# A gated mix of a long convolution and a token mixer on one core: halves of the token tensors loaded in pairs from one queue, zeros between tap products, and a new hand-written order

## The chip, the cores and the metric

The kernel runs on one core of a Trainium2 chip. TensorE (PE in the profile) multiplies matrices into PSUM; VectorE (DVE), ScalarE (ACT) and GpSimd (POOL) compute on SBUF and empty PSUM; SyncE (SP) computes nothing and issues most of the DMAs. The metric is the device time of one execution in microseconds (us), the median of several runs.

## The reference

Inputs are bf16, with S = 2048 tokens and D = 640 channels. x is the tensor q. Cut to what matters:

```python
g = sigmoid((x * gate_w).sum(-1, keepdims=True))
# branch a: a 4-tap shift convolution, a product, a convolution over all 2048 tokens, a gate by q
k_shift = sum over t of k_pad[:, t:t + S, :] * shift_k[:, 3 - t]
kv = k_shift * v
y  = irfft(rfft(kv padded to 2S) * rfft(ssm_k padded to 2S))[:S] + kv * ssm_D
a  = x * y
# branch b: a token-shift mixer and an MLP
h  = gelu(layernorm(x) @ w1)           # 640 -> 640
hs = concat(h shifted by +1, -1, +2, -2 tokens, a quarter of the channels each) @ w2
x1 = x + hs
b  = x1 + gelu(layernorm(x1) @ w3) @ w4    # 640 -> 1536 -> 640
out = g * a + (1 - g) * b
```

The long convolution is done as a Fourier transform in two steps, written as matrix products with small tables of sines.

## The kernel before, in words

Tokens lie on partitions in a folded way: token number is 32n + 16g + s, partition is 64g + n (g is 0 or 1), and s (0 to 15) counts "slots". So one slot is a tile of 128 tokens by 640 channels, and a load of some slots is made of two **halves**, g = 0 for partitions 0 to 63 and g = 1 for partitions 64 to 127, a DMA each.

`build` (line 354) writes the work as some 780 tasks. Each has an engine (or a choice of engines), the buffers that it takes and gives back, and a function that issues its instructions. The tasks are issued in the order of the list `ORDER`, written out by hand above the code: numbers of tasks, with a letter where the engine is chosen (a is ACT, v is DVE, p is POOL). Every engine and every queue works strictly in that order. `Plan.place` (line 147) goes through the same list with estimated costs, only to choose buffers and the number of **fills**: matmuls of zeros (line 255) into a spare bank that keep PE busy while it would wait.

The stages, with the names and lines of the kernel before:

- Head: tables of sines (POOL, DVE lines 414 to 447, ACT line 451). Tap weights are spread over partitions by PE (`cjb`, line 464, one partition's row times ones) and copied to SBUF (`cj`). x is loaded (`ldx`, line 476), its statistics are made on DVE (lines 513 to 515) or ACT (519, 520), finished on POOL (526 to 528), it is normalized (`nm1`, 532 or 534), transposed by PE (`tr1`, 540) and copied out of PSUM (`ev1`). The filter ssm_k is loaded in 5 blocks (`ldsk`, line 489) and transposed by PE (`trh`, line 754, 32 matmuls a block).
- First mixer: `w1` (615, 619) with gelu on ACT (632), `w2` (641), and `x1` on DVE (648), which adds to x.
- Tap stage, on DVE alone: for each of four groups of four slots (`kv3` first, `kv0` last) 4 products with tap weights (774), 3 sums (778) and the product with v (782): 8 passes over 2560 elements.
- First Fourier step: `s1h` on the filter and `s1x` on the four groups of kv (809, 822), copied to SBUF, written to DRAM and read back in another order (834, 848).
- MLP: layernorm of x1, transposed by DMA (`dt2`, 716), `w3` (724) with gelu (731), `w4` (738), `t2` on DVE (744).
- Second Fourier step and back: `s2` (856), products on DVE (871), `s3` (884), to DRAM and back (896, 916).
- End: `s4` (934), `yq` (940, times q, which is loaded again, 922), `ad` (946), store (955).

All loads and stores but six are on SP's queue; the six g = 1 halves of x are on ACT's. K is loaded in four pieces of 4 slots (`ldk`, 493), v likewise (`ldv`, 767), both as halves of 4 slots (320 KB each); x in halves of 2 or 4 slots. SP holds at most 8 DMAs in flight: each issue waits for the DMA eight issues before it.

PSUM has 8 banks; a fill keeps one bank until the first `w1`, and most tasks take a pair.

Of the kernel before, what the change touches and what calls it, by code (L numbers as in the profile page):

```python
# [10 lines left out]
ACT = mybir.ActivationFunctionType  # L11
ALU = mybir.AluOpType
BF16 = mybir.dt.bfloat16
# [3 lines left out]
P = 128  # L17
D = 640
# [18 lines left out]
0 4 3 17 20 19 63p 8 22 23 24 30 54v 28 73p 2 5 1 55 26 21 74v 64v 56a 18 37 33 57 59v 76a 77 66v 75 36 7 11 35  # L37
9 10a 13 79v 15 12a 58v 16a 390 14a 40 396 65 25 78v 80 67 82v 34 41 83 29 39 6 391a 68v 69v 81v 84a 60 62v 31
70 71v 86v 61a 394 397a 122 27 38 85 87v 32 92v 93 395a 88 90a 114v 126 123 115 42 89v 127 91 116v 100v 118v 47
398 392 130 45 399v 98a 124 117 101 131 94a 125 128 49 72v 95v 119v 43 99 129 96 106v 393a 97v 108v 400 120 132  # L40
107 102a 51 103a 133 109 121a 138 139 135 136 134 104 110v 441 111v 453 454a 141 442a 105v 112 142 44 144 449
403 455 48 113a 461 404 405 406 407 408 166 145 168 450a 172 462a 402 46 456a 169 173 443 444a 459 170 167 460a
146 401 171 53 174 152 445 147 447 457 175 153 52 409 414 410 148 458a 137 446a 448a 214 150 151 182 176 149 464
413 415 215 177 183 216a 463 179 180 140 157 451 452 185 143 217 465 473 158 220 163 181 186 159 474a 466a 188
471 416 189 412 164 411 469 477 196 50 221 470a 192 224v 225 218v 478v 472a 197 417 418 467 483 485 193 419 468a
190 486a 191 194 160 484a 154 420 481 161 219 476 165 479 475 195 198 222v 421 155 162 264 424 480a 482a 199 223
422 178 201 202 207 489 156 423 258 487 497 490a 265 208 302 210 211 259 262v 491 498a 268v 495 266a 488 492a
212 204 226 230 425 260a 501 205 213 496a 426 227 231 493 494a 509 242 701 303 261 712 244 236 502a 427 228 702
243 507 510a 245 500 304v 237 508a 713 505 263 503 428 504a 240 506a 429 232 499 269 241 267 434 233 229 246 238
248 430 433 435 513 517 436 437 511 438 431 432 247 239 249 515 516a 234 270 235 439 252 512 518a 514a 271 187  # L50
521 522a 305 519 520a 440 280 253 281 290 525 291 527 306v 526v 529 274 530a 531 528v 184 533 276 308 250 534a
206 200 532v 282 203 524 309 307 523 209 312v 310v 277 535 346 347 352 251 275 536 286 697v 256 283 313 311 353
356v 537 287 542 257 254 558 553 272 538 354a 543 348v 350a 255 539v 574 540 292 273 622 544a 559 541a 545 288
546a 278 289 560v 547 284 293 279 548 554 556 285 569 349 561 555v 557a 562a 563 564 585 590 294 575 576a 295
549 551v 314 355 550a 570 357 577 315 572 606 316 571v 573v 601 578a 317 591 593 649 592a 326 320 579 565 594a
327 324 586 580 321 566a 567v 325 588 589a 587v 552 336 607 595 351 337 602 596 604 605v 322 608a 318 603a 633
597 323 599v 609 617 328 618 319 598a 332 610a 620 568 329 611 623 612 334 624v 619a 654 681 650 651v 621a 333
652 625 626v 330 653a 335 581 331 582a 627 655 670 628 583a 342 656a 634 635a 613 343 636 657 614v 658v 638 639
600 615a 584 659 660 637a 629 641 640a 665 344 630a 616 642a 643 644 345 686 671 631a 632 672a 666 667v 668 687
688v 669a 689 682 684 685v 690a 661 683a 662a 645 663v 673 675 674a 646a 647a 676 298 691 677 648 299 698 678a  # L60
679a 692 664 693 680 694v 695a 296 300 340 301 297 699a 358 341 696 711 714 717 700 370 718 715 722 706 703 707
# [22 lines left out]
class Plan:  # L84
# [62 lines left out]
    def place(self, order):  # L147
        tasks = self.tasks
        n = len(tasks)
        free = {e: 0.0 for e in LAT}  # L150
# [5 lines left out]
        for i in order:  # L156
            t = tasks[i]
            e = t.on
# [63 lines left out]
def kernel(  # L222
# [16 lines left out]
    nc = tc.nc  # L239
# [8 lines left out]
    with tc.manual_schedule():  # L248
        nc.vector.memset(env.early("FZ", [P, 512], BF16)[:], 0.0)
# [104 lines left out]
def build(env, nc, io):  # L354
    pl = Plan()
    add = pl.add
# [17 lines left out]
    def dma(name, nbytes, fn, issue=0.58, queue="SP", **kw):  # L374
        return add(name, queue, issue, fn, nbytes=nbytes, **kw)
# [79 lines left out]
    fill = add("fill", "PE", 0.02, lambda t: None, acq=[ONE], mode="f")  # L455
# [18 lines left out]
    for (s0, s1) in [(14, 16), (0, 2), (2, 4), (4, 8), (8, 12), (12, 14)]:  # L474
        for g in range(2):
            dma(f"ldx{s0}.{g}", 64 * (s1 - s0) * D * BF * 1.2, lambda t, s0=s0, s1=s1, g=g: (nc.scalar if g else nc.sync).dma_start(
                out=env["x"][64 * g:64 * g + 64, s0:s1, :], in_=qv[g, :, s0:s1, :]), queue="ACT" if g else "SP",
                w=[("x", s, g) for s in range(s0, s1)])
# [12 lines left out]
    for (i0, i1) in ((15, 19), (11, 15), (7, 11), (3, 7)):  # L491
        for g in range(2):
            dma(f"ldk{i0}.{g}", 64 * (i1 - i0) * D * BF * HALF, lambda t, i0=i0, i1=i1, g=g: nc.sync.dma_start(
                out=env["K"][64 * g:64 * g + 64, i0:i1, :], in_=kv_[g, :, i0 - 3:i1 - 3, :]),
                w=[("K", i, g) for i in range(i0, i1)], roles=("K",))
    dma("ldkh1", 64 * 3 * D * BF * 2, lambda t: nc.sync.dma_start(out=env["K"][64:128, 0:3, :], in_=kv_[0, :, 13:16, :]),
        w=[("K", i, 1) for i in range(3)], roles=("K",))
    dma("ldkh0", 64 * 3 * D * BF * 2, lambda t: nc.sync.dma_start(out=env["K"][1:64, 0:3, :], in_=kv_[1, 0:63, 13:16, :]),
        w=[("K", i, 0) for i in range(3)], roles=("K",))
# [265 lines left out]
    for gi in (3, 2, 1, 0):  # L765
        for g in range(2):
            dma(f"ldv{gi}.{g}", 64 * 4 * D * BF * HALF, lambda t, gi=gi, g=g: nc.sync.dma_start(
                out=env["VC"][64 * g:64 * g + 64, 0, :, :], in_=vv[g, :, 4 * gi:4 * gi + 4, :]), w=[("V", g)], roles=("VC",))
# [144 lines left out]
    for s0 in range(0, 16, 2):  # L913
# [4 lines left out]
        qown = None  # L918
        for g in range(2):
            def ldq(t, s0=s0, g=g, o=qown):  # L920
                b = (o or t).buf["Q"][0]
                nc.sync.dma_start(out=env["QO"][64 * g:64 * g + 64, 2 * b:2 * b + 2, :], in_=qv[g, :, s0:s0 + 2, :])
            kw = dict(acq=("Q",), after=("W12",)) if qown is None else {}
            t = dma(f"ldq.{s0}.{g}", 64 * 2 * D * BF * HALF, ldq, use=[qown] if qown else [], w=[("q", s0, g)], **kw)
            qown = qown or t
        oown = None
        for i in range(2):
# [14 lines left out]
            y = add(f"yq.{s}", "DVE", 0.88, yq, use=[t], rel=[(t, "U"), (qown, "Q")], r=["GG", ("q", s0, 0), ("q", s0, 1)], acq=("V",),  # L942
# [6 lines left out]
            o = add(f"ad.{s}", "DVE", 0.75, ad, use=[y] + ([oown] if oown else []), rel=[(y, "V")], r=["GG", ("x", s, 0), ("x", s, 1)],  # L949
                    w=[("o", s)], after=("W12",), **kw)  # L950
            oown = oown or o
        for g in range(2):
            def st(t, s0=s0, g=g, o=oown):
                b = 4 + 2 * o.buf["O"][0]
                nc.sync.dma_start(out=ov[g, :, s0:s0 + 2, :], in_=env["QO"][64 * g:64 * g + 64, b:b + 2, :])
            dma(f"st.{s0}.{g}", 64 * 2 * D * BF * HALF, st, r=[("o", s0), ("o", s0 + 1)], rel=[(oown, "O")])
# [32 lines left out]
```

## Time and profile before

| | us |
|---|---|
| median of 3 runs (238.21 to 238.35) | 238.26 |
| the profiled execution, own time | 238.23 |
| its span, first to last instruction | 236.5 |
| PE, DVE, ACT, POOL busy | 220.1, 185.9, 158.2, 36.8 |
| first `w1` matmul / first tap pass / last tap pass ends | 27.01 / 45.60 / 109.36 |
| last `s1x` group starts on PE / last matmul ends about | 111.38 / 230.5 |

A line of the chain or of a timeline gives the start in us from the span's first instruction, the length, the engine, what it writes, its source line and the number of instructions merged. A line of the windows gives a stretch, its length, then for PE, PEld (weight loads), DVE, ACT and POOL the busy time and number of instructions in it, then PE's granted clock (1.00 is full), the mean busy share of the 16 DMA engines, and GB/s. A busy PE includes the fills.

### The profile page before, as it was taken

The page shows a single profiled execution, that of the slowest core. Times are in us where ns is not written, and L with a number is a line of the kernel's source. Part 1 is how long each engine was busy: PE and PEld are TensorE (multiplying, and loading weights), DVE is VectorE, ACT ScalarE, POOL GpSimd, SP SyncE. Part 2 cuts the span into 40 slices and gives each one's busy share as a digit, 9 for nine tenths or more (in the row PEclk, how much of TensorE's full clock was granted, in tenths as well). Part 3 has the DMA queues.
Part 4 walks back from the last instruction along what each step waited for, and adds up shares of the span by engine and source line. Part 5 has one row for each costly group of instructions (what it writes and reads, how often), then busy time and mean ns, then how long its engine had stood idle before and what let it go on. Part 6 is the DMA issues. An engine that isn't in the chain of part 4 may idle for free.

```text
span 236.5 us, 5276 instructions
## 1 busy us (share of the span) xinstructions
PE 220.1 (93%) x2135; PEld 109.7 (46%) x2154; DVE 185.9 (79%) x263; ACT 158.2 (67%) x221; POOL 36.8 (16%) x91
## 2 busy tenths in 40 slices
PE   8489799999999999999999999999879999999990
PEld 2147576634544564444554343334345654454550
DVE  6926696899999989996754888897999327787892
ACT  0995989998699797887963868897976702522000
POOL 8553364000530330000240000000000000000000
PEclk9679999999999989999999999999999999999997
DMA  6999999998998956985999699987851876877942
GB/s 169 206 224 286 288 214 194 229 335 309 358 243 197 257 199 160 271 236 149 320 259 387 205 237 276 259 283 269 262 192 36 316 258 238 294 218 244 266 112 55
DMA packets 37429, 56.23 MB, mean 238 GB/s; under 512 B 13467, under 2 KB 28572, under 8 KB 37404
## 3 DMA queue, kind: packets, MB, share of 16 engines
q1 hardware_dynamic: 36924, 54.57, 80.2%
q10 hardware_dynamic: 480, 1.31, 2.4%
q8 instruction: 17, 0.28, 0.5%
q14 instruction: 8, 0.07, 0.1%
HBM read 34.90 MB, written 18.35 MB: 225 GB/s over the span
## 4 chain that ended last, share of the span: by engine, by line
PE 76%; DMA 13%; DVE 3%; issue 2%; ACT 2%; SPq 1%; ACTq 0%; DVEq 0%
PE PS L724 23%; PE PS L738 16%; PE PS L641 9%; PE PS L615 8%; DMA x<-in_A_q_dram 6%; DMA W<-in_B_w_dram 5%; PE PS L884 4%; PE PS L856 4%; PE PS L809 4%; DMA QO<-in_A_q_dram 2%; PE PS L619 2%; PE PS L754 2%; PE PS L934 2%; DVE W L940 1%; PE PS L540 1%
## 5 line engine op out<-in xcount | busy, mean ns | idle before, releaser
L738 PE MATMUL PS<-W,h2T 128*128 128x128 bf16 (+1 forms) x372 | 53.6, 297 | 0.6
L731 ACT ACTIVATE h2T<-PS 128x512 bf16<-128x512 f32 x48 | 27.8, 605 | 29.6 <-PE PS L724 29.0
L738 PEld LDWEIGHTS <-h2T 128*128 128x128 bf16 x384 | 29.9, 98 | 25.9 <-issue 2.3
L379 ACT CAST FS<-PS 128x1024 bf16<-128x1024 f32 x36 | 35.1, 1017 | 3.6 <-PE PS L809 2.4
L724 PEld LDWEIGHTS <-W 128*128 128x128 bf16 x240 | 21.9, 99 | 30.2 <-issue 8.7
L379 ACT CAST XH<-PS 128x1024 bf16<-128x1024 f32 x26 | 25.6, 1018 | 5.9 <-PE PS L856 4.2
L724 PE MATMUL PS<-x1nT,W 128*128 128x512 bf16 x120 | 29.5, 392 | 0.0
L724 PE MATMUL PS<-XB,W 128*128 128x512 bf16 x120 | 28.3, 380 | 0.0
L774 DVE TENSOR_TENSOR VC<-K,VC 128x2560 bf16<-128x2560 bf16 x16 | 23.7, 1489 | 0.3
L871 DVE TENSOR_TENSOR PP<-XH 128x2048 bf16<-128x2048 bf16 x20 | 23.6, 1220 | 0.5 <-ACT XH L379 0.2
L744 DVE TENSOR_TENSOR x<-PS,x 128x640 bf16<-128x640 f32 x16 | 13.1, 822 | 13.4 <-PE PS L738 13.2
L641 PE MATMUL PS<-W,hsT 128*128 128x128 bf16 (+1 forms) x155 | 23.2, 302 | 0.3
L615 PE MATMUL PS<-xnT,W 128*128 128x512 bf16 x80 | 19.0, 380 | 0.4 <-DMA W<-in_B_w_dram 0.4
L698 POOL TENSOR_TENSOR r<-v,MH 128x2 f32<-128x2 f32 x8 | 8.9, 1107 | 64.7 <-DVE v L693 62.9
L381 DVE CAST XH<-PS 128x1024 bf16<-128x1024 f32 x14 | 16.8, 1221 | 2.7 <-PE PS L856 2.7
L778 DVE TENSOR_TENSOR VC<-VC 128x2560 bf16<-128x2560 bf16 x12 | 17.9, 1490 | 0.3
L940 DVE SCALAR_TENSOR_TENSOR W<-PS,GG,QO 128x640 bf16<-128x640 f32 x16 | 13.4, 880 | 6.0 <-PE PS L934 3.6
L641 PEld LDWEIGHTS <-hsT 128*128 128x128 bf16 x160 | 12.8, 100 | 11.5 <-issue 1.5
L379 ACT CAST GS<-PS 128x1024 bf16<-128x1024 f32 x14 | 13.9, 1016 | 3.2 <-PE PS L884 3.1
L856 PE MATMUL PS<-FX,TRIG 64*32 64x512 bf16 x320 | 12.9, 382 | 1.6 <-DVE GS L381 0.8
L648 DVE SCALAR_TENSOR_TENSOR x<-PS,x 128x640 bf16<-128x640 f32 x16 | 12.8, 819 | 1.0 <-PE PS L641 1.0
L946 DVE SCALAR_TENSOR_TENSOR QO<-x,OG,W 128x640 bf16<-128x640 bf16 x16 | 13.3, 879 | 0.1
(105 smaller groups left out, 266.8 us busy)
## 6 DMA issues: line engine op xcount, KB each, us to landing
FH<-FS SPq DMA_DIRECT2D x8, 640.0 KB, 5.6
FXD<-FS SPq DMA_DIRECT2D x8, 640.0 KB, 4.6
FX<-FH SPq DMA_DIRECT2D x10, 512.0 KB, 4.0
FX<-FXD SPq DMA_DIRECT2D x10, 512.0 KB, 6.0
GX<-GD SPq DMA_DIRECT2D x8, 640.0 KB, 5.2
W<-in_B_w_dram SPq DMA_DIRECT2D x2, 1920.0 KB, 17.4
GD<-GS SPq DMA_DIRECT2D x8, 480.0 KB, 3.7
SK<-in_A_ssm_k_dram SPq DMA_DIRECT2D x5, 512.0 KB, 7.6
```

The source lines that it names most:

```text
L379: nc.scalar.copy(out=out, in_=in_)
L381: (nc.vector if t.on == "DVE" else nc.gpsimd).tensor_copy(out=out, in_=in_)
L615: nc.tensor.matmul(m[:, b, :], lhsT=W[:, 0, kb, 160 * fb:160 * fb + 128], rhs=rhs(kb, shifts[fb]), start=(kb == 0), stop=(kb == 4))
L641: nc.tensor.matmul(m[:, c0:c1], lhsT=env["hsT"][:, o.buf["hs"][0], fb, 128 * (s % 4):128 * (s % 4) + 128], rhs=env["W12"][:, 1, fb, c0:c1] ...
L724: nc.tensor.matmul(env.PS[:, t.buf["U"][0], :], lhsT=env["W3"][:, kb, 128 * fb:128 * fb + 128], rhs=env.nT(int(nP[-1]))[:, :, kb, :], star ...
L731: nc.scalar.activation(out=env["h2T"][:, o.buf["h2"][0], fb, :], in_=env.PS[:, t.buf["U"][0], :], func=ACT.Gelu_apprx_tanh)
L738: nc.tensor.matmul(m[:, c0:c1], lhsT=env["h2T"][:, o.buf["h2"][0], fb, 128 * (s % 4):128 * (s % 4) + 128], rhs=env["W4"][:, fb, c0:c1], st ...
L774: nc.vector.tensor_tensor(out=VC[:, o], in0=env["K"][:, a + 3 - j:a + 7 - j, :], in1=w, op=ALU.mult)
L778: nc.vector.tensor_tensor(out=VC[:, 1], in0=VC[:, 1], in1=VC[:, 2], op=ALU.add)
L856: nc.tensor.matmul(env.U(t.buf["U"][0])[32 * j:32 * j + 32, gp, :], lhsT=CRI()[64 * gp:64 * gp + 64, 32 * pc:32 * pc + 32], rhs=X[64 * gp: ...
L871: nc.vector.tensor_tensor(out=env["PP"][:, o.buf["PP"][0], a, :].rearrange("p (b c) -> p b c", b=2), in0=X.unsqueeze(1).broadcast_to([P, 2 ...
L940: nc.vector.scalar_tensor_tensor(out=u, in0=env.Uf(t.buf["U"][0])[:, 0:D], scalar=SS("GG")[:, s:s + 1], in1=env["QO"][:, 2 * q.buf["Q"][0] ...
```

## The change

Five things are edited.

1. All halves go through one helper that issues g = 1 and then g = 0 back to back on SP, 2 slots (160 KB) each: x, K, v, the second load of q and the output. ACT issues no DMA any more. x, K and v so have 16 issues each in place of 12, 8 and 8.
2. Ahead of everything SP loads eight rows of w3 (72 KB), which the full load of w3 later writes again.
3. The load of K's shifted rows for g = 0 (63 rows) becomes 48 and 15 rows.
4. The memset of the zeros becomes a task behind one other memset, and at least one fill stands ahead of every `cjb` behind the first.
5. A new `ORDER` with other engine choices, and changed estimates in `place` (a half's cost 1.45 becomes 1.1 or 1.3).

```diff
-HALF = 1.45
+HALF = 1.1
...
+                    if self.kept is not None and t.name[:3] == "cjb":
+                        t.fill = max(t.fill, 1)
...
-        nc.vector.memset(env.early("FZ", [P, 512], BF16)[:], 0.0)
+        nc.sync.dma_start(out=env["W3"][0:8, 0:3, :], in_=B_w3[0:384].rearrange("(t p) n -> p t n", p=P)[0:8])
...
+    def halves(name, nbytes, out, in_, **kw):
+        def fn(t):
+            for g in (1, 0):
+                nc.sync.dma_start(out=out(t, g), in_=in_(t, g))
+        return add(name, "SP", 1.08, fn, nbytes=nbytes, **kw)
...
-    for (s0, s1) in [(14, 16), (0, 2), (2, 4), (4, 8), (8, 12), (12, 14)]:
-        for g in range(2):
-            dma(f"ldx{s0}.{g}", 64 * (s1 - s0) * D * BF * 1.2, lambda t, s0=s0, s1=s1, g=g: (nc.scalar if g else nc.sync).dma_start(
+    for s0 in (14, 0, 2, 4, 6, 8, 10, 12):
+        halves(f"ldx{s0}", P * 2 * D * BF * HALF, lambda t, g, s0=s0: env["x"][64 * g:64 * g + 64, s0:s0 + 2, :],
...
-    for (i0, i1) in ((15, 19), (11, 15), (7, 11), (3, 7)):
-        for g in range(2):
-            dma(f"ldk{i0}.{g}", 64 * (i1 - i0) * D * BF * HALF, lambda t, i0=i0, i1=i1, g=g: nc.sync.dma_start(
+    for i0 in (15, 17, 11, 13, 7, 9, 3, 5):
+        halves(f"ldk{i0}", P * 2 * D * BF * HALF, lambda t, g, i0=i0: env["K"][64 * g:64 * g + 64, i0:i0 + 2, :],
```

What the new order does on each engine, by the instructions of the two programs:

- PE does the same matmuls but for 5 more fills (34 for 29). Ahead of the first `w1` it now does all 5 `trh` blocks (before: 3) and 4 `tr1` (before: 3). Blocks 1 to 3 of `trh` stand in one run behind the four `cjb`, then 8 fills, two `tr1`, blocks 4 and 5, two `tr1`.
- SP starts with w3's rows, the pair x0, an SK block, the taps' row, the pairs x14 and x4, SK, x2, ssm_D, three more SK blocks, x6 and w1 (its 20th DMA); then a first pair of K, x8, x12, x10 and more of K. The first tap pass now reads slots that are complete with SP's 38th DMA, the second one slots that are complete with the 50th; up to there stand 10.07 MB, 5.67 MB of them in halves.
- DVE starts the first tap pass ahead of all `x1` (before: behind four of them). Between its first and last tap pass it has the 32 tap passes, 15 `x1`, 3 copies `ev1`, two statistics and small work.
- Behind the start of the last `s1x` group PE has 185 matmuls of `w3` and all 384 of `w4` left (before: 165 and 360), and the same of the rest. In the part with `s2` and `s3`, from the first `s2` to the last `s3`, it has 115 of `w3` and 96 of `w4` among them (before: 80 and 96).

More of the change, by code (lines that the diff above doesn't have):

```diff
@@ L149, in place @@
         n = len(tasks)
-        free = {e: 0.0 for e in LAT}
+        free = {e: 0.0 if e != "SP" else 0.58 for e in LAT}
         bufs = {p: [0.0] * k for p, k in self.pools.items()}
@@ L372, in build, with dma @@
         qv, kv_, vv, ov = tok(q2), tok(k2), tok(v2), tok(o2)
-    def dma(name, nbytes, fn, issue=0.58, queue="SP", **kw):
-        return add(name, queue, issue, fn, nbytes=nbytes, **kw)
+    def dma(name, nbytes, fn, issue=0.58, **kw):
+        return add(name, "SP", issue, fn, nbytes=nbytes, **kw)
+    def halves(name, nbytes, out, in_, **kw):
[3 more added lines that the diff above has]
+        return add(name, "SP", 1.08, fn, nbytes=nbytes, **kw)
     def copy(t, out, in_):
@@ L453, in build @@
     add("sin", "ACT", 3.5, c_sin, r=["pha", "c0"], w=["TRIG"], roles=("PRE", "C0"))
-    fill = add("fill", "PE", 0.02, lambda t: None, acq=[ONE], mode="f")
+    zeros = add("zeros", "DVE", 0.3, lambda t: nc.vector.memset(env.early("FZ", [P, 512], BF16)[:], 0.0), roles=("C0",))
+    fill = add("fill", "PE", 0.02, lambda t: None, use=[zeros], acq=[ONE], mode="f", roles=("C0",))
     dma("ldCJ", 5120, lambda t: nc.sync.dma_start(out=env.early("CJR", [1, 4 * D], BF16), in_=io["sk"].rearrange("d j -> (d j)").unsqueeze(0)),
@@ L471, in build @@
                                                   in_=io["gw"].rearrange("(t p) -> p t", p=P)), w=["GW"])
-    for (s0, s1) in [(14, 16), (0, 2), (2, 4), (4, 8), (8, 12), (12, 14)]:
-        for g in range(2):
-            dma(f"ldx{s0}.{g}", 64 * (s1 - s0) * D * BF * 1.2, lambda t, s0=s0, s1=s1, g=g: (nc.scalar if g else nc.sync).dma_start(
-                out=env["x"][64 * g:64 * g + 64, s0:s1, :], in_=qv[g, :, s0:s1, :]), queue="ACT" if g else "SP",
-                w=[("x", s, g) for s in range(s0, s1)])
+    for s0 in (14, 0, 2, 4, 6, 8, 10, 12):
+        halves(f"ldx{s0}", P * 2 * D * BF * HALF, lambda t, g, s0=s0: env["x"][64 * g:64 * g + 64, s0:s0 + 2, :],
+               lambda t, g, s0=s0: qv[g, :, s0:s0 + 2, :], w=[("x", s, g) for s in (s0, s0 + 1) for g in range(2)])
     dma("ldw1", 819200, lambda t: nc.sync.dma_start(out=env["W12"][:, 0], in_=io["w1"].rearrange("(t p) n -> p t n", p=P)),
@@ L490, in build, with kh0 @@
             w=[("SK", cb)], roles=("SK",))
-    for (i0, i1) in ((15, 19), (11, 15), (7, 11), (3, 7)):
-        for g in range(2):
-            dma(f"ldk{i0}.{g}", 64 * (i1 - i0) * D * BF * HALF, lambda t, i0=i0, i1=i1, g=g: nc.sync.dma_start(
-                out=env["K"][64 * g:64 * g + 64, i0:i1, :], in_=kv_[g, :, i0 - 3:i1 - 3, :]),
-                w=[("K", i, g) for i in range(i0, i1)], roles=("K",))
-    dma("ldkh1", 64 * 3 * D * BF * 2, lambda t: nc.sync.dma_start(out=env["K"][64:128, 0:3, :], in_=kv_[0, :, 13:16, :]),
+    for i0 in (15, 17, 11, 13, 7, 9, 3, 5):
+        halves(f"ldk{i0}", P * 2 * D * BF * HALF, lambda t, g, i0=i0: env["K"][64 * g:64 * g + 64, i0:i0 + 2, :],
+               lambda t, g, i0=i0: kv_[g, :, i0 - 3:i0 - 1, :], w=[("K", i, g) for i in (i0, i0 + 1) for g in range(2)], roles=("K",))
+    dma("ldkh1", 64 * 3 * D * BF * HALF, lambda t: nc.sync.dma_start(out=env["K"][64:128, 0:3, :], in_=kv_[0, :, 13:16, :]),
         w=[("K", i, 1) for i in range(3)], roles=("K",))
-    dma("ldkh0", 64 * 3 * D * BF * 2, lambda t: nc.sync.dma_start(out=env["K"][1:64, 0:3, :], in_=kv_[1, 0:63, 13:16, :]),
-        w=[("K", i, 0) for i in range(3)], roles=("K",))
+    def kh0(t):
+        nc.sync.dma_start(out=env["K"][1:49, 0:3, :], in_=kv_[1, 0:48, 13:16, :])
+        nc.sync.dma_start(out=env["K"][49:64, 0:3, :], in_=kv_[1, 48:63, 13:16, :])
+    dma("ldkh0", 64 * 3 * D * BF * HALF, kh0, issue=1.08, w=[("K", i, 0) for i in range(3)], roles=("K",))
     dma("ldw3", 1966080, lambda t: nc.sync.dma_start(out=env["W3"][:], in_=io["w3"].rearrange("(t p) n -> p t n", p=P)), w=["W3"])
@@ L765, in build @@
     for gi in (3, 2, 1, 0):
-        for g in range(2):
-            dma(f"ldv{gi}.{g}", 64 * 4 * D * BF * HALF, lambda t, gi=gi, g=g: nc.sync.dma_start(
-                out=env["VC"][64 * g:64 * g + 64, 0, :, :], in_=vv[g, :, 4 * gi:4 * gi + 4, :]), w=[("V", g)], roles=("VC",))
+        for h in range(2):
+            halves(f"ldv{gi}.{h}", P * 2 * D * BF * HALF, lambda t, g, h=h: env["VC"][64 * g:64 * g + 64, 0, 2 * h:2 * h + 2, :],
+                   lambda t, g, gi=gi, h=h: vv[g, :, 4 * gi + 2 * h:4 * gi + 2 * h + 2, :], w=[("V", h)], roles=("VC",))
         a = 4 * gi
@@ L917, in build @@
         ld = dma(f"rG.{s0}", P * 5120, rg, issue=0.5, r=[("G", m) for m in range(10)], acq=("GX",), after=("FX",))
[L918 to L925, printed above, removed]
+        qown = halves(f"ldq.{s0}", P * 2 * D * BF * 1.3, lambda t, g: env["QO"][64 * g:64 * g + 64, 2 * t.buf["Q"][0]:2 * t.buf["Q"][0] + 2, :],
+                      lambda t, g, s0=s0: qv[g, :, s0:s0 + 2, :], acq=("Q",), w=[("q", s0)], after=("W12",))
         oown = None
@@ L941, in yq @@
                                                in1=env["QO"][:, 2 * q.buf["Q"][0] + i, :], op0=ALU.mult, op1=ALU.mult)
[L942 removed]
+            y = add(f"yq.{s}", "DVE", 0.88, yq, use=[t], rel=[(t, "U"), (qown, "Q")], r=["GG", ("q", s0)], acq=("V",),
                     after=("C0",))
@@ L948, in build @@
             kw = dict(acq=("O",)) if oown is None else {}
-            o = add(f"ad.{s}", "DVE", 0.75, ad, use=[y] + ([oown] if oown else []), rel=[(y, "V")], r=["GG", ("x", s, 0), ("x", s, 1)],
+            o = add(f"ad.{s}", "DVE", 0.88, ad, use=[y] + ([oown] if oown else []), rel=[(y, "V")], r=["GG", ("x", s, 0), ("x", s, 1)],
                     w=[("o", s)], after=("W12",), **kw)
             oown = oown or o
[L952 to L956, printed above, removed]
+        halves(f"st.{s0}", P * 2 * D * BF * 1.3, lambda t, g, s0=s0: ov[g, :, s0:s0 + 2, :],
+               lambda t, g, o=oown: env["QO"][64 * g:64 * g + 64, 4 + 2 * o.buf["O"][0]:6 + 2 * o.buf["O"][0], :],
+               r=[("o", s0), ("o", s0 + 1)], rel=[(oown, "O")])
     pl.close()
```

50 lines of the change are left out of this document (25 added, 25 removed), and 8 rows, old and new, of the table ORDER.

## The prediction

> **What bounds the kernel now.** I read the page's busy shares first (PE 93%, DVE 79%), then the chain of waits, then windows and DVE's timeline. The chain is PE almost without a break from the first `w1` on, and what lets PE begin is the load of w1:
>
> ```profile
> 16.20 10.76 DMA W<-in_B_w_dram
> 27.01 1.25 PE PS L615 x5
> 29.90 3.70 PE PS L754 x64
> 111.38 0.76 PE PS L809 x6
> 231.43 0.88 DVE QO L946
> ```
>
> These are pieces of the chain, in order of time. To see: w1 lands at 26.96; two of the five filter blocks are transposed only behind it (64 matmuls, 3.70 us); the last `s1x` group starts at 111.38; after PE's last matmul (about 230.5) come `t2`, `ad` and the store, 6.0 us to the span's end at 236.5.
>
> DVE is a second bound in the middle, which its windows and timeline show:
>
> ```profile
> 50.00:60.00 10.00, 9.95 (x83) 4.13 (x83) 9.73 (x10) 9.03 (x15) 0.53 (x1) 1.00 0.91 332
> 90.00:100.00 10.00, 10.00 (x58) 4.22 (x57) 9.83 (x9) 8.78 (x13) 0.00 (x0) 1.00 0.82 219
> ```
>
> ```profile
> 45.60 2.89 DVE L774 TENSOR_TENSOR VC<-K,VC 128x2560 bf16<-128x2560 bf16 x2
> 107.87 1.49 DVE L782 TENSOR_TENSOR K<-VC 128x2560 bf16<-128x2560 bf16 x1 [0.88 <-DMA VC<-in_A_v_dram]
> ```
>
> To see: DVE is 97 and 98% busy while it works through the tap passes, from 45.60 to 109.36, and PE's last `s1x` group, which needs the last of them, follows 2.0 us later. Up to 40 us DVE was busy for 27.2 us only (sum of the windows); 12.8 us lay idle.
>
> The loads, by windows of the head:
>
> ```profile
> 3.00:4.00 1.00, 1.00 (x4) 0.31 (x3) 0.94 (x1) 0.00 (x0) 1.00 (x1) 1.00 1.10 264
> 9.00:10.00 1.00, 0.00 (x0) 0.00 (x0) 0.93 (x4) 0.97 (x3) 0.85 (x2) 0.50 0.97 236
> 23.00:24.00 1.00, 0.44 (x6) 0.29 (x3) 0.99 (x2) 0.66 (x1) 0.17 (x1) 1.00 1.05 373
> 36.00:38.00 2.00, 2.00 (x25) 1.50 (x24) 0.35 (x1) 1.64 (x4) 1.05 (x3) 1.00 0.99 218
> ```
>
> To see, in the last two columns: the DMA engines are full in all of them (share about 1), yet halves of K behind each other move 218 GB/s (30 to 40 us: 210) while w1, on 128 partitions, moves 373. At 3 us halves of x come from both queues at once: 264, and 243 as the mean of 2 to 5 us. And PE idles at 9 us, at clock 0.50.
>
> **The change, part by part.**
>
> *Pairs of halves.* From the rows I take whole loads at 360 GB/s (373 and its neighbours) and bound halves by 210 (one half after the other) and 315 (SP's issue: 160 KB per 0.52 us, the median issue of x's halves being 0.51). I take 300, near the upper end: the rows with both halves under way are above 210 even at the start; and eight rows ahead, which is few for 16 engines, may set some engines behind the others, so that at any time both halves are being written (no trace of before shows it). The first transfer begins at 2.3; with 0.5 us for the end, SP's 50th DMA has landed at 2.8 + 4.4 MB/0.36 + 5.67 MB/0.30 = 33.9 us (at 210: 42.0). w1, at 5.20 MB with 1.64 in halves, lands at 2.8 + 9.9 + 5.5 = 18.2, no longer what PE waits for.
>
> The Trainium skill, in "SBUF — State Buffer", section "Can I just issue two DMAs to hit both halves?", speaks against this: two transfers are not fused, so each half keeps its own eight ports. The 218 GB/s row agrees for halves in sequence; the 264 row doubts it for two at once. By that rule the sum is that of the second rival.
>
> *Head on PE.* Zeros start 0.1 us later and 5 more are 5 x 0.216 (the spacing of full-clock 512-column matmuls) = 1.1 us. The fourth tap product waits for PSUM until a copy frees a pair, as in the trace (3.5 us there, for ACT's copy); ACT, free of issues, begins at about 4.7 (the first halves landed at 4.5 before) rather than 5.57, so its copy ends at 10.3. Rows 8 to 14 show the clock halved after such a wait; I charge one `trh` block at half speed, 3.4 us, and 1.85 us (3.70 / 2) for each other. Then: product 4 to 11.1, a fill, blocks 1 to 3 to 18.4, 8 fills to 20.1, two `tr1` of 0.56 and a fill to 21.4, blocks 4 and 5 with a fill to 25.4, two `tr1` and four fills to 27.4. **First `w1` at 27.4**, with 64 `trh` and 10 `tr1` matmuls (3.7 + 0.56 us) already done that were behind it.
>
> *Head on DVE.* Tables until 5.7 (the rows' own sum), x14 at 7.0, statistics, mask, a PSUM copy (0.8, as `x1`) and norms to 16.7; the third filter block is copied only when PE has it, 18.4 to 19.7; `tr1` copies and norms, each behind its PE step, to 32.2. There the first tap pass starts, 13.4 us earlier than now; the second, behind two copies, statistics and norms of 4.2 us, at 37.9, and its K is there at 33.9: 4.0 us of cover.
>
> *DVE through the taps.* 32 passes in four groups of 12.1 us (starts 1.52 apart) = 48.4; 15 `x1` of 0.83 = 12.5; 3 copies 2.4; two statistics 2.3; norms and small ones 2.8: 68.4 us. Idle between: before, 3.7 us in 40 to 110; bounds 0.5 and 6, I take 2.3 as data come earlier. **The last tap pass ends at 32.2 + 68.4 + 2.3 = 102.9** (before: 109.36), and the last `s1x` group starts at 103.0, as PE would wait for it: on its own it would be there at 27.4 + 69.8 (its matmuls at the rows' spacing) + 1.7 (the half-clock weight loads behind `gate`, 87.3 to 89.8, gate being kept) = 98.9.
>
> *PE behind it.* Before: 230.5 - 111.4 = 119.1 us, of which the matmuls at the rows' spacing make 115.3 and stalls and small gaps 3.8. After: 20 more `w3` matmuls (5 in 1.09) and one more `w4` (24 in 3.31) = +7.7, so 123.0. Of the 3.8 most (22.0 - 19.74 = 2.3 us) lies in 164 to 186, where the order has no `w3` between `s2`, `s3` and `w4`; the new one has 35 more `w3` matmuls in that stage. I take 1.5 off (bounds 0 and 2.3, or 3 more where the copies, DVE 91% and ACT some 80% busy there, fall behind): 2.3 left.
>
> *Nearly nothing:* 28 more SP issues (some 14 us of SP, hidden as the transfers are longer), ACT's six issues gone (4.8 us, ahead of its first data), the split of 63 rows, copies swapped between ACT and DVE (about 1 us each way). In the tail pairs may spare 0 to 0.5 us of the last store; I take 0, so 6.0.
>
> **Sum:** 103.0 + 123.0 + 2.3 + 6.0 = 234.3 us of span, 2.2 less than 236.5. The profiled execution took 238.23 with 1.73 outside its span, the median is 238.26: **236.0 us**.
>
> **The rivals.**
>
> *PE, not DVE, sets the middle:* the clock is not halved (the zeros between products keep it), DVE waits little and pairs hold 300. PE's group at 97.5: 97.5 + 123.0 + 2.3 + 6.0 + 1.73 = **230.5**. For it: DVE's bare sum from 32.2 ends at 100.6, from 29 at 97.4. Against it: DVE's 98% windows.
>
> *Slower: the second tap pass waits for K.* If halves keep 210 GB/s, K lands at 42.0, 4.1 us behind DVE's 37.9; everything in DVE's queue (`x1`, copies that free PSUM) stands behind that pass, and PE behind those. The last group starts at 107.1, the time is **240.1**. It decides below 226 GB/s for halves, where that pass starts after 40.1 and the 2.2 us are gone. For it: the 218 row. A clock cold through all three `trh` blocks (3.1 us) has the same effect by the same queue.
>
> The Trainium skill ("TensorE: Matmul & The Clock Gate", Part 1) has the clock halve after an idle window of about 3.4 us; the trace agrees with 3.45 us idle before 11.09 and clock 0.50 around it. By that rule the zeros spare a cold block, 1.6 us of the head, and the sum would be 234.4.
>
> *The change does less than it says:* the engines fall back into step, pairs get some 230, the order's gain and its later work cancel: about **238**.
>
> **How the numbers follow.** Forecast and its surroundings (233 to 237.6) 0.44, PE-bound 0.20, no difference 0.07, slower 0.29 (waits for K, cold clock, or copies late in the `s2` stage). 0.2% is about what a measurement of this kernel can tell from no change. Faster so has 0.64. The range 230.5 to 241 takes in the first rival's value and the bounds of DVE's idle (102.9 - 1.8, + 3.7) and of the later stalls.
>
> **What would show it.** K pairs near 300 GB/s in the windows of 20 to 35 us; the first tap pass near 32 and the second near 38, waiting for no DMA; first `w1` near 27; last tap pass near 103 with PE waiting for it; less PE idle in the last third of the `s2` stage. Wrong, if the second tap pass waits for K, if the clock is low from 11 to 17 us, or if PE idles 4 us or more behind 120 us.

## The result, and the profile after

The changed kernel takes **240.7 us** (median of 14 runs, 238.56 to 244.65) where the kernel before takes 237.75 (14 runs beside them): a ratio of 1.013, interval 1.0091 to 1.0169. It is slower, by 1.3%; I had said 236.0 and faster. In a second series the ratio was 1.019 (1.0129 to 1.0249). The profiled execution took 241.77 us, its span is 239.9. Single executions of one kernel spread by 2 to 3%, the ratios leave out the slowest, and the profiled execution of d0 below was such a slow one, so that only its times up to the last `s1x` group are read.

The head of TensorE is as forecast; the first `w1` stands at 27.40. The middle is not. From VectorE's and TensorE's timelines of the changed kernel (in brackets: idle time ahead of the instruction and what ended it):

```profile
36.52 1.49 DVE L785 TENSOR_TENSOR VC<-K,VC 128x2560 bf16<-128x2560 bf16 x1 [4.73 <-DMA K<-in_A_k_dram]
46.23 1.49 DVE L785 TENSOR_TENSOR VC<-K,VC 128x2560 bf16<-128x2560 bf16 x1 [3.01 <-DMA K<-in_A_k_dram]
105.65 1.49 DVE L793 TENSOR_TENSOR K<-VC 128x2560 bf16<-128x2560 bf16 x1
```

```profile
27.40 2.32 PE L626 MATMUL PS<-xnT,W 128*128 128x512 bf16 x10
107.20 0.60 PE L820 MATMUL PS<-K,TRIG 64*128 64x512 bf16 x4 [0.34 <-DVE K L793]
```

To see: VectorE reached the first tap pass at 31.8 (36.52 - 4.73; forecast 32.2) and stood there until its K landed. The second pass waited for K again and began at 46.23 (forecast 37.9). The last one ends at 107.14 (forecast 102.9), and TensorE's last `s1x` group follows at 107.20. That is 4.2 us sooner than before (111.38), but 132.7 us follow it, where 125.1 did (236.5 - 111.38): the order has put some 7.7 us of `w3` and `w4` behind it. 7.6 - 4.2 = 3.4 us of span lost.

Why K is late shows in the chain of waits (start, length, what)

```profile
14.16 10.48 DMA W<-in_B_w_dram
24.66 0.47 SPq L385
...
34.58 4.95 DMA K<-in_A_k_dram
39.55 6.59 DMA K<-in_A_k_dram
...
46.23 1.50 DVE VC L785
```

in SP's timeline, which lists the DMAs issued (L489 is w1, L482 gate's weights of 1.2 KB, L495 a block of w2 of 40 KB, L385 the halves of 160 KB), and in the line of SP's own waits for the loads of weights (us in total, times, longest):

```profile
14.16 0.40 SPq L489 DMA_DIRECT2D W<-in_B_w_dram  x1
14.61 0.53 SPq L482 DMA_DIRECT2D GW<-in_gate_w_dram  x1
15.34 1.55 SPq L385 DMA_DIRECT2D K<-in_A_k_dram  x2
17.07 0.45 SPq L495 DMA_DIRECT2D W<-in_B_w_dram  x1
19.09 1.11 SPq L385 DMA_DIRECT2D x<-in_A_q_dram  x2
20.48 1.21 SPq L495 DMA_DIRECT2D W<-in_B_w_dram  x1
24.66 3.48 SPq L385 DMA_DIRECT2D x<-in_A_q_dram  x4
```

```profile
SPq L385 <- DMA W<-in_B_w_dram: 6.2, 2, 3.2
```

To see: SP holds 8 DMAs in flight. Behind w1 stand seven, three of them tiny; the next, a half of x, may go only when w1 has landed, at 24.66. By then nearly all bytes of the seven have been moved too (5.9 MB in all), so the DMA engines run dry. The windows show it (stretch, length, then PE, PEld, DVE, ACT, POOL, and last the clock, the DMA share and GB/s):

```profile
18.00:24.00 6.00, 6.00 (x76) 4.47 (x73) 5.17 (x12) 5.29 (x8) 2.33 (x7) 1.00 1.09 238
24.00:28.00 4.00, 4.00 (x55) 3.16 (x54) 2.86 (x6) 3.19 (x6) 2.05 (x6) 1.00 0.34 98
28.00:42.00 14.00, 10.45 (x81) 4.64 (x80) 8.27 (x20) 9.98 (x14) 3.26 (x9) 0.91 0.97 254
42.00:46.00 4.00, 4.00 (x41) 1.65 (x40) 0.82 (x1) 2.78 (x5) 1.41 (x5) 0.90 0.63 161
```

In these windows full DMA engines move 238 to 254 GB/s, and in 24 to 28 us they are a third busy. The pair of K with slots 11 and 12 is SP's 49th and 50th DMA; its second half is issued at 39.55 and takes 6.6 us to land. Ahead of it stands w2's first load (640 KB, issued at 35.22, landed at 43.2), and there SP stops a second time: the 51st DMA goes only then. These two stops are the 6.2 us of the line of waits, and in 42 to 46 us the engines are 0.63 busy.

From 32 to 36 us nothing but halves is under way in either kernel. The kernel before, then the changed one:

```profile
32.00:36.00 4.00, 4.00 (x56) 2.51 (x55) 3.91 (x9) 3.38 (x8) 2.96 (x8) 1.00 1.02 207
32.00:36.00 4.00, 3.25 (x30) 1.46 (x29) 0.00 (x0) 4.00 (x7) 0.48 (x2) 1.00 0.97 261
```

So halves do move faster than before, but not at 300 GB/s.

### The profile page after: what moved, and what is told of

Same layout as the page of the kernel before. It is cut to its first block, busy times and chain, and to the rows that moved or that the text cites. A ratio compares the mean times of both kernels' runs of the same rounds, so it can differ in the third digit from the quotient of the medians.

```text
span 239.9 us, 5342 instructions
## 1 busy us (share of the span) xinstructions
PE 224.4 (94%) x2159; PEld 108.5 (45%) x2159; DVE 186.7 (78%) x262; ACT 157.2 (66%) x224; POOL 40.9 (17%) x90
## 4 chain that ended last, share of the span: by engine, by line
PE 58%; DMA 18%; DVE 13%; SPq 6%; issue 2%; DVEq 0%
PE PS L749 21%; PE PS L735 14%; SPq L385 5%; DMA K<-in_A_k_dram 5%; PE PS L867 5%; PE PS L652 5%; DMA W<-in_B_w_dram 4%; DVE VC L789 4%; PE PS L895 4%; PE PS L626 4%; DVE VC L785 4%; DMA GX<-GD 4%; DMA x<-in_A_q_dram 3%; DMA FX<-FH 2%; DVE x L659 2%
## 5 line engine op out<-in xcount | busy, mean ns | idle before, releaser
L749 PE MATMUL PS<-W,h2T 128*128 128x512 bf16 (+1 forms) x384 | 53.9, 300 | 0.0
L390 ACT CAST FS<-PS 128x1024 bf16<-128x1024 f32 x38 | 37.3, 1023 | 3.5 <-PE PS L820 2.5
L735 PEld LDWEIGHTS <-W 128*128 128x128 bf16 x240 | 21.0, 98 | 30.4 <-issue 9.2
L390 ACT CAST XH<-PS 128x1024 bf16<-128x1024 f32 x25 | 24.9, 1014 | 9.4 <-PE PS L867 8.4
L735 PE MATMUL PS<-x1nT,W 128*128 128x512 bf16 x120 | 28.2, 380 | 0.0
L652 PE MATMUL PS<-W,hsT 128*128 128x512 bf16 (+1 forms) x160 | 23.4, 300 | 2.3 <-DVE x L659 2.2
L392 DVE CAST XH<-PS 128x1024 bf16<-128x1024 f32 x15 | 18.2, 1221 | 3.8 <-PE PS L867 2.6
L626 PE MATMUL PS<-xnT,W 128*128 128x512 bf16 x80 | 20.2, 397 | 0.0
L709 POOL TENSOR_TENSOR r<-v,MH 128x2 f32<-128x2 f32 x8 | 7.8, 979 | 65.8 <-DVE v L704 56.6
L643 ACT ACTIVATE hsT<-PS 128x512 bf16<-128x512 f32 x20 | 11.7, 617 | 6.7 <-PE PS L626 6.4
```

What stands on the lines that cost most here:

```text
L390: nc.scalar.copy(out=out, in_=in_)
L392: (nc.vector if t.on == "DVE" else nc.gpsimd).tensor_copy(out=out, in_=in_)
L626: nc.tensor.matmul(m[:, b, :], lhsT=W[:, 0, kb, 160 * fb:160 * fb + 128], rhs=rhs(kb, shifts[fb]), start=(kb == 0), stop=(kb == 4))
L652: nc.tensor.matmul(m[:, c0:c1], lhsT=env["hsT"][:, o.buf["hs"][0], fb, 128 * (s % 4):128 * (s % 4) + 128], rhs=env["W12"][:, 1, fb, c0:c1] ...
L735: nc.tensor.matmul(env.PS[:, t.buf["U"][0], :], lhsT=env["W3"][:, kb, 128 * fb:128 * fb + 128], rhs=env.nT(int(nP[-1]))[:, :, kb, :], star ...
L749: nc.tensor.matmul(m[:, c0:c1], lhsT=env["h2T"][:, o.buf["h2"][0], fb, 128 * (s % 4):128 * (s % 4) + 128], rhs=env["W4"][:, fb, c0:c1], st ...
```

## The experiments

My theory: the time is lost because K comes late through SP's queue, by its place on the queue, by w1 holding the ring, and by issues of 160 KB; VectorE's order then holds everything up. Rivals: halves in pairs are slow by themselves; the new order is worse whatever the loads do; the copies blocked behind the first tap pass, and TensorE's clock, are the cost. What all runs gave (us; the ratio is to the kernel before, on the same chip):

| kernel | first tap pass | second | last `s1x` group | span | ratio (interval) |
|---|---|---|---|---|---|
| changed | 36.52 | 46.23 | 107.20 | 239.9 | 1.013 (1.009 to 1.017) |
| the same again | 35.47 | 46.09 | 108.72 | 241.1 | 1.019 (1.013 to 1.025) |
| a1, no eight rows | 35.63 | 46.27 | 108.87 | 240.7 | 1.021 (1.017 to 1.025) |
| a2, K by 4 slots | 35.85 | 41.76 | 104.14 | 237.1 | 1.004 (0.999 to 1.008) |
| a3, small loads later | 32.42 | 41.94 | 102.96 | 235.2 | 1.005 (1.001 to 1.009) |
| a4, first tap pass later | 38.75 | 45.89 | 109.14 | 241.1 | 1.020 (1.016 to 1.025) |
| b1, a2 and a3 | 35.90 | 42.95 | 105.37 | 238.7 | 1.007 (1.002 to 1.012) |
| b2, b1 and V later | 33.78 | 39.23 | 102.63 | 234.9 | 0.999 (0.995 to 1.003) |
| c1, b1 with runs of halves | 35.12 | 41.27 | 103.59 | 235.9 | median 239.88 to 237.56, no interval |
| d0, K11 sooner | 34.69 | 41.50 | 104.66 | not read | 1.000 (0.995 to 1.005) |
| d1, d0 and a3 | 33.28 | 38.54 | 101.58 | 234.0 | **0.990** (0.986 to 0.994) |
| d2, d1 and V later | 31.88 | 38.22 | 99.92 | 232.5 | **0.989** (0.985 to 0.994) |
| d3, d1 without the zeros | 33.21 | 38.47 | 99.83 | 235.8 | 0.997 (0.993 to 1.001) |

The times and the span are of one execution each. The two traces of the changed kernel differ by 1.2 us in span and by 1.5 us in the last group, so a difference of that size between two traces shows nothing; the ratios rest on several executions each.

**a1: the eight rows alone.**

```diff
-        nc.sync.dma_start(out=env["W3"][0:8, 0:3, :], in_=B_w3[0:384].rearrange("(t p) n -> p t n", p=P)[0:8])
```

> The changed kernel without its first transfer of eight rows of w3, so that the first pair of halves starts on idle DMA engines. Theory 1 (the time is lost because K reaches VectorE late through SP's queue: w1's landing holds the ring of 8, small loads fill its slots, and back-to-back issues of 160 KB are slower than the transfers; the pairs themselves are fast): if the eight rows matter for the pairs, the windows from 3 to 7 us fall from 279 to 322 GB/s to some 210 to 250 and the x loads land up to 2 us later; if they do not, these windows stay near 300. In both cases w1's landing (24.66 us) and the second tap pass (46.23) move by less than 1.5 us, so the time is 240 to 242 us. Rival (halves in pairs are slow by themselves, rows or not): the windows of 3 to 7 us are the same with and without the rows, at or below 250.

Windows of 2 to 8 us, of the changed kernel and of a1:

```profile
2.00:8.00 6.00, 5.87 (x18) 1.87 (x16) 3.95 (x15) 2.89 (x5) 3.83 (x9) 1.00 0.86 250
```

```profile
2.00:8.00 6.00, 6.00 (x16) 1.82 (x15) 4.20 (x15) 3.33 (x6) 4.06 (x10) 1.00 0.92 259
```

250 and 259 GB/s, and by single microseconds from 3 to 7 us 279 to 322 with the rows and 251 to 363 without: setting engines apart by eight rows does nothing for the pairs. The time (242.6 us, just above the 240 to 242 expected) is within the interval of the changed kernel in its second series.

**a2: K in halves of 320 KB** (the loads named 17, 13, 7 and 5 in the code bring 4 slots each, the other four nothing).

```diff
+    K4 = {17: 15, 13: 11, 7: 7, 5: 3}
...
+        if i0 in K4:
+            a = K4[i0]
+            halves(f"ldk{i0}", P * 4 * D * BF * HALF, lambda t, g, a=a: env["K"][64 * g:64 * g + 64, a:a + 4, :],
```

> The changed kernel with K loaded in halves of 4 slots (320 KB), four pairs in place of eight at the places of the first pairs: 8 issues of SP fewer, the same bytes. Theory 1 (SP's issues of 0.635 us for each 160 KB half bound the rate after w1 has landed): the windows of 28 to 36 us rise from 241 to 265 GB/s to about 300, K is complete for the second tap pass 3 us sooner, the second wait of a tap pass for K (3.0 us) is gone or below 1 us, the last tap pass ends at 104 to 105 in place of 107.15, and the time falls by 2 to 3 us to some 238. Rival (halves are limited by their ports at about 210 to 260 GB/s, whatever their size): the rate in those windows stays below 265 GB/s, both waits stay, the time is 240 to 241. Rival 3 (the order is worse behind the last s1x group, whatever the loads do): the last tap pass moves but the time does not follow.

The second wait is gone, the last pass ends at 104.1 and the ratio falls to 1.004, as expected. The reason that I gave was only half right: in 30 to 38 us the rate did not rise to 300; the windows show 251, 266, 243 and 243 GB/s at a DMA share of 0.98 to 1.04. Issues of 160 KB each 0.635 us (258 GB/s) happen to be about as slow as the halves themselves. What helped is that the ring behind w1 held 640 KB of K (238 GB/s in 24 to 28 us for 98), and that slots 11 and 12 came with 13 and 14. The three small loads still stand behind w1 here: it is more bytes behind w1 that fill this window.

**a3: the three small loads later.**

```diff
-28 19 40 30 25 32 26 27 47 39 398 42
+28 40 25 26 27 47 39 398 42 19 30 32
```

(tasks of SP in `ORDER`: 28 is w1, 19 gate's weights, 30 and 32 blocks of w2, 25 to 27 x, 42 the pair of K with slots 13 and 14.)

> The changed kernel with three loads of little data (gate's weights, 1.2 KB, and two blocks of w2) moved on SP's queue from their places between w1 and the first loads behind it to behind the third pair of K; nothing else is moved. Theory 1 (while w1's landing holds the ring of 8, the bytes in flight run out, since three of the seven slots behind it hold little): the windows of 24 to 28 us rise from 127, 66, 154 and 47 GB/s to a mean above 200, the first tap pass starts about 2 us sooner than 36.52, and the second wait for K shrinks by 1 to 2 us; the time falls by 1 to 2 us, or by less if gate and w2 now come late. Rival (w1 itself is slow to move, or the rate is limited by the halves): the windows of 24 to 28 us stay below 120 on the mean, the time is 240 to 241.

```profile
24.00:28.00 4.00, 4.00 (x55) 3.20 (x54) 2.85 (x6) 3.19 (x6) 1.99 (x6) 1.00 0.91 228
```

The window that showed 98 GB/s now shows 228, the first tap pass starts 4.1 us sooner and the second 4.3. Together with a2, where these loads stayed and K's halves grew, this shows the ring that held few bytes to be a cause. In the other traces with the old ring (the same again, a1, a4, d0) this window has 127, 177, 212 and 164 GB/s, in a2, b1, d1 and d2 236 to 261. A shorter dip comes where the three loads stand now (140 GB/s in 30 to 32 us). The second wait for K did not shrink, as I had expected (3.75 us, before the edit 3.01). The span falls by 4.7 us, but a3's traced execution lies 2.4 us below the median of its runs; the ratio falls to 1.005, by 0.8% from the first series and 1.4% from the second.

**a4: only the first tap pass moved**, behind copies out of PSUM that stood behind it (task 401 behind 102).

> The changed kernel with only VectorE's first tap pass moved, behind the third of the copies out of PSUM that stand behind it in VectorE's queue, so that these copies no longer wait for K. Theory 1 (the second tap pass's K at 46.2 us is what times the chain of tap passes): TensorE's idle time of 3.6 us before the s1h matmuls and the granted clock of 0.85 in 38 to 50 us vanish, but the second tap pass still waits for K until about 46, the last tap pass ends at 106 to 107.5 and the time changes by less than 1 us (240 to 241). Rival 4 (the blocked copies, TensorE's idle time and its clock are what costs): the time falls by 3 us or more, to 237.7 or less.

TensorE's waits, of the changed kernel and of a4 (us in total, times, longest), and a window of a4:

```profile
PE PS L820 <- DVE xnT L392: 3.6, 1, 3.6
PE PS L652 <- DVE x L659: 2.2, 1, 2.2
```

```profile
PE PS L651 <- DVE x L658: 5.8, 1, 5.8
```

```profile
40.00:50.00 10.00, 7.83 (x59) 3.41 (x53) 4.28 (x4) 9.16 (x16) 4.46 (x7) 1.00 0.86 243
```

The wait of 3.6 us is gone and the clock is 1.00 in this window (0.86 in the changed kernel); the second pass still starts at 45.89, TensorE idles 5.8 us at `w2` instead, its clock is 0.51 from 52 to 59 us, and nothing is gained (the last pass ends at 109.1, expected 106 to 107.5). While K is late, the blocked copies (VectorE's; only VectorE and ScalarE empty PSUM in these traces, GpSimd does not) and the low clock are only moved. So the rival that they cost the time by themselves falls.

**b1, b2, c1: both edits, V later, and pairs taken apart.** b2 moves task 398 behind 42. c1 issues slots 8 to 13 of x as three halves g = 1 and then three g = 0:

```diff
+            for s0 in (8, 10, 12):
+                nc.sync.dma_start(out=env["x"][64 * g:64 * g + 64, s0:s0 + 2, :], in_=qv[g, :, s0:s0 + 2, :])
```

> The changed kernel with both edits that brought K sooner: K in halves of 4 slots, and the three small loads behind the third pair of K. Theory 1 (K on SP's queue is the cause, and both edits act on it): the first tap pass starts at 32 to 33, the second at 38 to 39 without a wait for K (41.9 and 41.8 with one edit alone), the last tap pass ends at 98 to 100, the last s1x group follows, and behind it lie the same 132 to 133 us as in the changed kernel (107.2 to 239.9): a span of 230 to 233 and a ratio to before of 0.980 to 0.995. Rival (the order has a second bound just below, such as TensorE's own head, so that a sooner K moves only idle time): the last tap pass ends at 100 or later or TensorE's group no longer waits for it, and the span stays at 234 to 236.

> The kernel with both edits, and the first pair of V moved behind the piece of K that stands behind it on SP's queue. Theory 1: K for both first tap passes is there 1.2 to 1.5 us sooner (two halves of 160 KB at 250 GB/s), which is worth at most what is left of the waits for K, 0 to 1 us; V is needed only at the eighth pass of the group and stays hidden. Rival (V becomes the wait): the product with V waits for a DMA and the time rises by up to 1 us.

> The kernel with both edits, in which three neighbouring pairs of x (slots 8 to 13) are issued as a run of three g = 1 halves and then a run of three g = 0 halves; bytes, sizes and places on the queue are the same. Theory 2 (a half alone is limited by its own partitions, and only two different halves side by side move more than 220 GB/s): the windows in which these runs move (about 19 to 25 us) fall from some 240 GB/s to 180 to 215, K lands 0.7 to 1.2 us later, and the time rises by up to 1 us. Rival (pairing does nothing; halves move at the same rate in any sequence): these windows stay at 230 to 250 GB/s and the times agree within 0.3%.

> The changed kernel itself, beside the others on the same chip, as their measure. All theories: a ratio to before of 1.009 to 1.017, the second tap pass near 46 us waiting for K, the last tap pass ending near 107, and 132 to 133 us from the start of the last s1x group to the span's end.

b1 missed: its first tap pass starts at 35.90, not 32 to 33, after a wait of 4.4 us for K. That pass reads slots 13 to 16; the piece of 4 slots that has 13 and 14 also brings 11 and 12, and behind two halves of V it lands later than the piece of two did. So the edits do not add. b2, with V behind it, gains 2.1 us on that pass and 3.7 on the second, more than the 0 to 1 us expected: the rival (V late) did not come. The same again gave 1.019, a little above the 1.009 to 1.017 expected. Windows in which mostly these six halves of x move, b1 (pairs) and c1 (runs):

```profile
24.00:27.00 3.00, 3.00 (x46) 2.46 (x43) 1.86 (x6) 2.54 (x5) 1.40 (x5) 1.00 1.06 267
```

```profile
23.00:26.00 3.00, 3.00 (x46) 2.66 (x46) 2.28 (x8) 2.97 (x4) 0.88 (x2) 1.00 1.06 230
```

In one trace each the runs move 230 GB/s and the pairs 267 (b2's pairs: 257 in 24 to 27 us); over 18 to 26 us the kernels show 259 and 260, but there w1 moves too. So pairing may be worth up to a sixth of the rate, and neither order is near 300. The time does not show it (medians 239.88 and 239.5). What exactly makes halves faster than the 207 of the kernel before stays open: a2's pairs of 320 KB, the size that K had before, move 243 in 34 to 38 us.

**d0 to d3: the late K itself.** d0 moves one task of SP: 41, the pair of K with slots 11 and 12, from behind 43, 46, 29, 48, 399 and 31 (K, w2, K's shifted rows, V) to right behind 42. d1 adds a3's move, behind 41; d2 moves 398 (V) behind 41 as well; d3 is d1 without the rule of the zeros:

```diff
-                    if self.kept is not None and t.name[:3] == "cjb":
-                        t.fill = max(t.fill, 1)
```

> The changed kernel with one task moved on SP's queue: the pair of K with slots 11 and 12, which completes K for the second tap pass, stands right behind the pair with slots 13 and 14 instead of behind two more pairs of K, the first load of w2, K's shifted rows and a pair of V. Theory 1 (the second tap pass is late because its K is the 50th DMA): the second tap pass loses its wait of 3.0 us and starts at about 43.2, the first one stays near 36.5, the last tap pass ends at 104.2, and with the 132 to 133 us behind the last s1x group the span is 236 to 238 and the ratio to before 1.000 to 1.008. Rival (any edit on SP's queue shifts the waits elsewhere, here to w2's first load): TensorE waits for that load and the ratio stays at 1.010 to 1.019.

> The same, and the three small loads behind that pair of K as well. Theory 1: the first tap pass starts near 32.4 as with the small loads alone, the second near 38.2 without a wait for K, the last tap pass ends at 98 to 99.5, and with 132 to 133 us behind the last s1x group the span is 230 to 233, the ratio to before 0.975 to 0.990. This is the time that the prediction gave (234.3 of span) or better. Rival (VectorE or TensorE has another bound that takes over): the last tap pass ends at 101 or later, the span is 234 or more.

> The same, with the first pair of V behind these pairs of K too. Theory 1: no wait for K is left for it to remove but some 0.6 us of the first tap pass; the span is that of the kernel before within 0.8 us. Rival (V now comes late for the first product with it): up to 1 us more.

> The kernel with the pair of K and the small loads moved, without the rule that puts at least one matmul of zeros ahead of each tap product behind the first. The zeros of the change were to keep TensorE's clock up in the head. If they do: the granted clock from 8 to 16 us is lower without them, the first w1 matmul comes 0.5 to 2 us later, and the time rises by 0 to 1 us. If they do not (the wait for a copy out of PSUM lets the clock fall with and without them): the clock in 9 to 16 us is about 0.50 in both, the head on TensorE is 0 to 1 us shorter, and the time agrees within 0.3%.

One task moved takes the ratio from 1.013 (1.019) to 1.000, with a last pass that ends at 104.60 (expected 104.2): this is the strongest of the proofs. d1 and d2 beat both kernels. VectorE's timeline of d1, then of d2:

```profile
33.28 1.49 DVE L784 TENSOR_TENSOR VC<-K,VC 128x2560 bf16<-128x2560 bf16 x1 [1.33 <-DMA K<-in_A_k_dram]
38.54 1.48 DVE L784 TENSOR_TENSOR VC<-K,VC 128x2560 bf16<-128x2560 bf16 x1
```

```profile
31.88 1.49 DVE L784 TENSOR_TENSOR VC<-K,VC 128x2560 bf16<-128x2560 bf16 x1
38.22 1.48 DVE L784 TENSOR_TENSOR VC<-K,VC 128x2560 bf16<-128x2560 bf16 x1
```

The waits are 1.33 us, and none; d2 stands where the forecast had put the changed kernel (32.2 and 37.9). Its last group, however, waits for VectorE still, by 0.34 us. d1's last pass ends at 101.5, later than the 98 to 99.5 expected, and its span of 234.0 lies at the border of the rival (another bound): from the second to the end of the last pass VectorE takes 63.0 us, in the changed kernel 60.9, so some 2 us of what K gave are lost again between the passes. VectorE idles 3.2 us there, in the changed kernel 1.4: it waits 0.8 us for V at 68.4 us, and 1.2 us in three waits for `w2` from TensorE, whose clock is 0.50 from 57.6 to 61.0 us. For d2 I expected no more than 0.8 us less than d1; the span is 1.5 less and the ratios agree. Without the zeros (d3) the first `w1` comes at 27.25, in d1 at 27.56, so they do not shorten the head. They do not hold the clock either: without them it is 1.00 from 8 to 12 us and 0.57 from 12 to 16, with them (d1) 0.56 from 9 to 16. Neither of my two cases had that. Behind the group d3 takes 136.0 us, d1 132.4: ahead of `s4` TensorE waits 2.3 us for the read-back (d1: 0.5), and from 213.5 to 216.9 us its clock is 0.50, which by my estimate (half of 3.4 us) costs 1.7. The head does not explain that later read-back, and I leave it open. The ratios, 0.990 and 0.997, have intervals that overlap slightly.

## Why the prediction was wrong, step by step

- **Head on PE: right in the number, partly by luck.** First `w1` at 27.4 and 27.40; `trh` blocks 1 to 3 until 18.1 (forecast 18.4). The forecast charged 3.4 us for one block at half clock. The three took 5.56 us, 1.85 each, though the clock was 0.50 for the first half of it (lines in the last section). But they began at 12.60, not 11.3, behind more zeros at half clock and a wait of 0.6 us for the filter's load. The two errors cancel. So the cold clock, a price in two of the rivals, costs these blocks nothing here.
- **Head on DVE: right.** Ready for the first tap pass at 31.8 (32.2).
- **Pairs of halves: the step that failed**, "SP's 50th DMA has landed at 33.9". K for the second pass landed at 46.1. In the sum the rate was mis-sized: full engines moved 238 to 254 GB/s, halves alone 261, not 300 for halves with 360 for whole loads. Neither the eight rows (a1), nor runs for pairs (c1), nor halves of 320 KB (a2) bring it there. By 18 us 4.37 MB had moved (sum of the windows); the other 5.70 MB at 254 take 22.4 us, which gives 40.4. For the remaining 5.7 us I had no term. Most of it is SP's ring: I had drawn a steady stream, but the queue stops until w1 has landed, with 2.5 us lost in 24 to 28 us (98 for 254 GB/s), and again behind w2, with 1.5 us lost in 42 to 46 (161). Another 0.4 us lies in 18 to 24 (238), and some 1.3 us are bytes from further back that moved beside K (10.39 MB had moved by 46 us).
- **w1 "lands at 18.2, no longer what PE waits for":** it landed at 24.66, since what stands behind it is moved beside it: 5.9 MB had moved by then, and w1 ends at 5.20. PE indeed did not wait, but SP's ring did.
- **"28 more SP issues, hidden":** not quite. After 24.66 SP issues back to back, at 0.59 + 0.04 us for a half (0.52 in the forecast), that is 258 GB/s at most: no margin over the transfers, but no bound of its own either (a2).
- **DVE through the taps: right in sum, not in its terms.** From the start of the first pass to the end of the last one it is 70.6 us, forecast 70.7. But VectorE was busy for 64.9 of them (forecast 68.4) and idle for 5.7 (2.3), 3.0 of that the wait for K. In d2 it is 68.0.
- **PE behind the last group: right in sum.** 132.7 us to the end, forecast 131.3. In 164 to 186 us all idle time has gone (22.00 busy of 22.00, before 19.74), as the order of `w3` there should do; a new wait of 1.1 us for a read-back stands ahead of it.
- **The second rival is what came**: "the second tap pass waits for K", 240.1 us, with the last group at 107.1 (measured 240.7 and 107.20). Its point of decision was set wrong: it should decide below 226 GB/s for halves, and full engines moved more than that. The wait came from the queue's stops as much as from the rate. That the number fits is luck in part: K came at 46.1, not 42.0, and from the second pass to the end of the last one VectorE took 60.9 us, not 65.0. The Trainium skill, "SBUF — State Buffer", "Can I just issue two DMAs to hit both halves?", has two transfers serialize; the traces bear that out in part only, with 257 and 267 GB/s for pairs, 230 for runs and 207 for the halves of before. By that rule the sum would have been this rival's.
- **The change can be faster than before**: with K in time (d1, d2) the span is 234.0 and 232.5, the forecast 234.3, and the ratios are 0.990 and 0.989, the forecast's 236.0 to 238.26 is 0.991. So the rest of the order was costed rightly in sum, and what takes its gain is which DMA stands where.

## What to carry to other kernels

When a queue allows a fixed number of DMAs in flight, count the bytes behind each big load: a load that takes 10 us with little behind it stops the stream, and only a landing restarts it. Place each transfer by the first instruction that reads it (here slots 11 and 12 of K ahead of slots 5 to 8, which had stood before them), and forecast a landing from the queue's order and its stops, not from bytes by an average rate. When an engine is blocked by a late load, look first at the load: here (a4) moving work around the blocked instruction only moved the idle time.

## What the runs showed of the hardware that was not expected

The clock fell without an idle time. TensorE in the head of the changed kernel, the timeline and two windows of it:

```profile
8.26 0.72 PE L476 MATMUL PS<-C,ONE 1*128 1x512 bf16 x2
8.91 1.89 PE L258 MATMUL PS<-C 128*128 128x512 bf16 x4
```

```profile
8.00:9.00 1.00, 1.00 (x5) 0.23 (x5) 0.97 (x4) 0.97 (x4) 0.69 (x2) 0.84 0.81 228
9.00:10.00 1.00, 1.00 (x3) 0.34 (x4) 1.00 (x1) 0.97 (x4) 1.00 (x1) 0.50 1.00 305
```

TensorE is busy from 1.20 to 12.0 us but for 0.13 us, and from 9 us the granted clock is 0.50; four zeros take 1.89 us (1.04 in d2 at full clock). In d2 the same stretch had 1.00 until 13 us, and 0.50 then from 14 to 17. The kernel before shows it too, where the prediction read the fall as coming after a wait:

```profile
7.00:8.00 1.00, 0.63 (x3) 0.20 (x3) 0.96 (x2) 0.97 (x3) 0.36 (x1) 0.91 0.79 171
8.00:9.00 1.00, 0.00 (x0) 0.00 (x0) 1.00 (x2) 0.97 (x3) 0.23 (x1) 0.50 1.11 165
```

TensorE's wait of 3.45 us there runs from 7.6 to 11.09 us. A mean of 0.91 in 7 to 8 us puts the fall to 0.50 at about 7.8, so it came as the wait began. The Trainium skill ("TensorE: Matmul & The Clock Gate", Part 1) has the clock halve after an idle window of about 3.4 us; in both kernels it halved without one, in a stretch that mixes one-row products with the zeros. So the agreement that the prediction saw is not there. What sets the moment no run here shows.

Half clock did not slow the filter's transposes. The three blocks of the changed kernel, and a window at each clock:

```profile
12.60 5.56 PE L765 MATMUL PS<-ID,SK 128*64 128x128 bf16 x96 [0.59 <-DMA SK<-in_A_ssm_k_dram]
```

```profile
13.00:14.00 1.00, 1.00 (x24) 1.00 (x22) 0.00 (x0) 0.99 (x2) 0.84 (x3) 0.50 1.00 284
16.00:17.00 1.00, 1.00 (x24) 1.00 (x22) 0.96 (x5) 1.00 (x1) 0.82 (x3) 1.00 1.14 298
```

24 matmuls and 22 weight loads fall into each microsecond, at 0.50 as at 1.00, while zeros of 512 columns take nearly twice the time.
